# Loading 128 rows in place of 96 for the values of a pair of heads

## The chip, the cores and the metric

The kernel runs on one core of one Trainium2 chip. The metric is the device time of one execution in microseconds (us); a lower time is better. The engines are PE (TensorE, matmuls), PEld (its weight loads), DVE (VectorE), ACT (ScalarE), POOL (GpSimd) and SP (SyncE, which issues all DMA transfers here).

## The reference

Local attention with block summaries, then a feed-forward layer in fp32. Batch 4, 8 heads, 768 tokens, head size 64; 512 model features, 2048 hidden.

```python
k_sum = k.reshape(B, H, nb, block, D).max(axis=3)      # block = 32, nb = 24
v_sum = v.reshape(B, H, nb, block, D).mean(axis=3)
mask_l = np.abs(pos[:, None] - pos[None, :]) < window  # window = 16
scores_s = scale * einsum('bhsd,bhnd->bhsn', q, k_sum) + np.log(block)
a = softmax(concatenate([where(mask_l, scores_l, -1e9), scores_s]))
x = matmul(a, concatenate([v, v_sum]))                 # -> (3072, 512)
h = x @ w_in
g = where(h >= 1, h, where(h <= -1, 0, (h + 1) ** 2 / 4))
out = g @ w_out
```

The weights come as 64-bit floats, 8 MB for each of the two matrices.

## The kernel before

The 3072 tokens are cut into 8 chunks of 384 tokens, c = 0 to 7: two halves for each of the 4 batch entries. Each chunk has 4 pairs of heads, p = 0 to 3. A step is named by a letter and its numbers: v02 is the load of the values of chunk 0, pair 2; F213 is a first-layer product of chunk 2.

For a pair, queries come in blocks of 64, six to a chunk. A block looks at a window of 96 keys (its own 64 and 16 on each side) and at 24 block summaries, 120 in all (KA = 120, KW = 96). The values lie in a tile `v` of 128 partitions by 6 blocks by 128 columns (two heads of 64): partitions 0 to 95 hold the windows and come by a DMA load (load_vals, v, L206 to L208), partitions 96 to 119 hold the 24 means, and partitions 120 to 127 are not read. The means are made on the chip: raw values come by another load (y, L203), DVE sums them (Y, L229), PE turns them (Z, L233), ACT copies them to the first block's columns of partitions 96 to 119 (mean_vals, V, L237), and POOL spreads them over the other five blocks (spread_vals, W, L241). Only then can PE multiply values by weights (values, A, L300). The host lays the windows out in `vwin`, an array of (batch, pair, half, 96, 6, 128) fp32 numbers; a load takes a contiguous piece of 96 rows of 3,072 bytes.

Keys are alike: window keys for chunk 0 are cut on the chip from raw keys (r, L178); for the later chunks they are loaded (k, L184), and POOL writes the summaries beside them (C, L225), so it waits for the load. Scores are S (L253), masks M (L261), exponentials E (L271), reciprocals D (L276), norms N (L281), transposes T (L286), copies of these P (L293), the split of a result into two fp32r parts X and L (L309, L314).

The feed-forward part takes 16 slices of 128 hidden features. Its weights come by 32 loads (w, L105 and L108) of 512 KB; ACT, DVE and POOL convert them to pairs of fp32r numbers (a at L120, b at L125, c at L133 to L141, d at L146 and L148, e at L154). First-layer products are F (L324), the activation G, H, I, J, O (L330 to L349), second-layer products B (L358).

What sets the order: chunk 0, all weight loads and conversions and the scores of chunk 1 are written out by hand as a list of steps (OPENING), which every engine follows. After it, PE's order is given by loops, and the other engines follow a scheduler. `v` tiles have 2 buffers (the loads of pairs 2 and 3 of chunk 0 go to a place in a weight buffer called `first`), so a later load waits until PE has used the values two pairs before. All DMA transfers are issued by SP in one row; the framework gives them eight semaphores in turn (named DMAHW0 to DMAHW7), and each transfer waits for the one eight places before it to land. An instruction that reads or overwrites what a load writes waits for that load's semaphore; regions that don't overlap make no wait.

Of the kernel before, what the change touches and what calls it, by code (L numbers as in the profile page):

```python
# [19 lines left out]
P = 128  # L20
# [4 lines left out]
KW = QB + 2 * WIN  # L25
KA = KW + NSUM
NPAIR = H // 2
T = 384
NHALF = S // T
# [44 lines left out]
def fused_kernel(ctx: ExitStack, tc: tile.TileContext, q2, kT, kwin, vT, vwin, w_in, w_out, mask, ident, out):  # L74
    nc = tc.nc
# [21 lines left out]
    def room(i, what, shape, dtype):  # L97

        return wpool.tile(shape, dtype, tag=f"w{i}", name=f"{what}{i}")
# [58 lines left out]
    q_ts, k_ts, v_ts, s_pss, es, dens, t_pss, pts, vs_pss, o_pss, xs = ({} for _ in range(11))  # L158

    def input_tile(pool, what, shape, c, p):  # L160
        if c == 0 and (what, p) in at_first:
            return at_first[what, p]
        tag, bufs = ("w", W_BUFS) if pool is stage else (what, {"k": K_BUFS, "q": Q_BUFS, "v": 2}[what])
        return pool.tile(shape, F32, tag=tag, name=f"{what}{c}_{p}", bufs=bufs)
# [3 lines left out]
    for i, share in enumerate(FIRST):  # L168
        at, at_room = 0, room(NF - 1 - i, "first", [P, 4 * DM], F32)
# [35 lines left out]

    def load_vals(c, p):  # L206
        v_ts[c, p] = input_tile(load, "v", [P, NB, P], c, p)
        nc.sync.dma_start(out=v_ts[c, p][:KW], in_=vwin[c // NHALF, p, c % NHALF])  # L208

    def window_keys(c, p):  # L210

# [161 lines left out]
    def load_constants():  # L373
# [5 lines left out]

    steps = {  # L380
        "m": load_constants, "r": load_raw_keys, "k": load_keys, "q": load_queries, "y": load_raw_vals, "v": load_vals, "w": fetch,
        "K": window_keys, "R": sum_keys, "C": summary_keys, "S": scores, "M": masks, "E": exps, "D": reciprocals, "N": norms,
        "T": transposes, "P": turned, "Y": sum_vals, "Z": turn_vals, "V": mean_vals, "W": spread_vals, "A": values, "X": high, "L": low,
# [122 lines left out]
```

## Time and profile before

| | |
|---|---|
| median of 3 runs | 663.87 us (662.9 to 664.74) |
| the profiled execution | 663.65 us |
| its span, first to last instruction | 661.8 us |
| busy: PE, ACT, POOL, DVE | 631.8, 370.3, 263.6, 254.9 us |
| granted TensorE clock, mean | 0.992 |
| DMA traffic | 63.55 MB, 96 GB/s over the span |
| loads of values, 288 KB each | 32, two of them to `first` |

The profile shows one execution. Times in it count from its first instruction. A row of a timeline gives start, duration, engine, line, operation, output<-input, count, and in brackets the idle time before it and what ended that wait. A row of the chain gives start, duration and what the time went to. A row of a window gives the window, its length, the busy time of PE, PEld, DVE, ACT and POOL with the count of instructions, the granted clock, the mean busy share of the 16 DMA engines, and GB/s. SPq is SP's own instruction that issues a transfer; the transfer itself lands later.

### The profile page before, as it was taken

The page shows a single profiled execution, that of the slowest core. Times are in us where ns is not written, and L with a number is a line of the kernel's source. Part 1 is how long each engine was busy: PE and PEld are TensorE (multiplying, and loading weights), DVE is VectorE, ACT ScalarE, POOL GpSimd, SP SyncE. Part 2 cuts the span into 40 slices and gives each one's busy share as a digit, 9 for nine tenths or more (in the row PEclk, how much of TensorE's full clock was granted, in tenths as well). Part 3 has the DMA queues.
Part 4 walks back from the last instruction along what each step waited for, and adds up shares of the span by engine and source line. Part 5 has one row for each costly group of instructions (what it writes and reads, how often), then busy time and mean ns, then how long its engine had stood idle before and what let it go on. Part 6 is the DMA issues. An engine that isn't in the chain of part 4 may idle for free.

```text
span 661.8 us, 11703 instructions
## 1 busy us (share of the span) xinstructions
PE 631.8 (95%) x4448; PEld 557.3 (84%) x4448; DVE 254.9 (39%) x494; ACT 370.3 (56%) x948; POOL 263.6 (40%) x300
## 2 busy tenths in 40 slices
PE   3779998899999999999999999999999999999997
PEld 2568787788898888899888888988888998889996
DVE  5879899362123322243222321235222122211111
ACT  3779897454546555464555545565554655544332
POOL 3569888343333332333333233234323323322221
PEclk9979999989999999999999999999999999999999
DMA  9999970370114121062122410254111100000001
GB/s 308 312 307 292 300 225 1 127 209 17 37 53 149 53 53 53 24 216 58 53 53 64 138 29 25 53 169 127 53 53 33 59 19 19 1 37 12 1 1 48
DMA packets 49767, 63.55 MB, mean 96 GB/s; under 512 B 24880, under 2 KB 33328, under 8 KB 49712
## 3 DMA queue, kind: packets, MB, share of 16 engines
q1 hardware_dynamic: 49712, 62.81, 32.0%
q8 instruction: 35, 0.57, 0.4%
q14 instruction: 20, 0.16, 0.1%
HBM read 56.51 MB, written 6.29 MB: 95 GB/s over the span
## 4 chain that ended last, share of the span: by engine, by line
PE 84%; DMA 9%; DVE 4%; ACT 1%; SPq 1%; issue 1%; POOL 0%; DVEq 0%; ACTq 0%
PE h L324 37%; PE acc L358 37%; PE o_ps L300 3%; DMA raw<-in_w_in 3%; PE s_ps L253 3%; PE t_ps L286 3%; DMA first<-in_vwin 2%; DMA q<-in_q 2%; DMA v<-in_vwin 1%; DMA first<-in_kT 1%; DVE w L141 1%; DVE c L133 1%; DVE c L136 1%; SPq L108 0%; DVE t L339 0%
## 5 line engine op out<-in xcount | busy, mean ns | idle before, releaser
L324 PE MATMUL h<-xhi,halves 128*128 128x384 f32 x1024 | 291.2, 343 | 6.6 <-DVE t L339 5.5
L358 PE MATMUL acc<-halves,ghi 128*128 128x512 f32 x768 | 239.8, 394 | 0.0
L349 POOL TENSOR_TENSOR glo<-t,ghi 128x384 fp32r<-128x384 f32 x128 | 129.5, 1013 | 203.2 <-ACT ghi L344 202.4
L324 PEld LDWEIGHTS h<-xhi,halves 128*128 128x128 f32 x1024 | 189.0, 189 | 17.0 <-issue 4.7
L339 DVE SCALAR_TENSOR_TENSOR t<-h,t 128x384 f32<-128x384 f32 x128 | 71.1, 556 | 270.8 <-ACT t L336 263.5
L324 PE MATMUL h<-xlo,halves 128*128 128x384 f32 x512 | 173.2, 338 | 0.0
L358 PEld LDWEIGHTS acc<-halves,ghi 128*128 128x128 f32 x768 | 144.7, 188 | 27.5
L358 PE MATMUL acc<-halves,glo 128*128 128x512 f32 x384 | 153.9, 401 | 0.1
L330 ACT ACTIVATE t<-h,ones_half 128x384 f32<-128x384 f32 x128 | 73.9, 578 | 121.7 <-PE h L324 121.2
L271 ACT ACTIVATE e<-e,den 128x120 f32<-128x120 f32 x192 | 73.4, 384 | 55.6 <-DVE den L266 55.6
L324 PEld LDWEIGHTS h<-xlo,halves 128*128 128x128 f32 x512 | 97.1, 190 | 4.5
L344 ACT CAST ghi<-t 128x384 fp32r<-128x384 f32 x128 | 65.4, 512 | 62.0 <-DVE t L339 61.8
L358 PEld LDWEIGHTS acc<-halves,glo 128*128 128x128 f32 x384 | 72.4, 189 | 12.5 <-issue 0.8
L281 POOL TENSOR_TENSOR e<-e,den 128x360 f32<-128x360 f32 x64 | 49.2, 789 | 56.0 <-ACT t L330 40.1
L336 ACT ACTIVATE t<-t 128x384 f32<-128x384 f32 x128 | 67.2, 526 | 3.6
L154 POOL TENSOR_TENSOR halves<-w,halves 128x1024 fp32r<-128x1024 f32 x16 | 38.5, 2408 | 3.0 <-ACT halves L148 2.1
L225 POOL COPY k<-ks 128x144 f32<-128x144 f32 x30 | 9.1, 305 | 74.5 <-DMA k<-in_kwin 70.6
L241 POOL COPY v<-v 24x640 f32<-24x640 f32 x30 | 21.5, 717 | 43.0 <-issue 33.3
L271 ACT ACTIVATION_READ_ACCUMULATOR e<-e,den 128x1 f32 x192 | 36.1, 188 | 0.0
L314 DVE TENSOR_TENSOR xlo<-o_ps,xhi 128x384 fp32r<-128x384 f32 x32 | 17.7, 554 | 46.4 <-ACT xhi L309 46.4
L300 PEld LDWEIGHTS o_ps<-pt,v 120*64 120x64 f32 x720 | 24.7, 143 | 12.1 <-ACT ghi L344 7.9
L261 DVE SCALAR_TENSOR_TENSOR e<-s_ps,mask_sb 128x360 f32<-128x360 f32 x64 | 30.9, 523 | 7.1 <-PE s_ps L253 6.8
(54 smaller groups left out, 421.2 us busy)
## 6 DMA issues: line engine op xcount, KB each, us to landing
k<-in_kwin SPq DMA_DIRECT2D x28, 360.0 KB, 4.3
v<-in_vwin SPq DMA_DIRECT2D x30, 288.0 KB, 3.1
raw<-in_w_in SPq DMA_DIRECT2D x16, 512.0 KB, 10.2
raw<-in_w_out SPq DMA_DIRECT2D x16, 512.0 KB, 10.1
out<-o SPq DMA_DIRECT2D x24, 256.0 KB, 2.1
q<-in_q SPq DMA_DIRECT2D x56, 96.0 KB, 4.1
kraw<-in_kT SPq DMA_DIRECT2D x13, 384.0 KB, 3.8
vraw<-in_vT SPq DMA_DIRECT2D x13, 384.0 KB, 3.8
```

Source lines behind the costliest of these rows:

```text
L154: nc.gpsimd.tensor_tensor(out=lo, in0=converting[i].bitcast(F32), in1=hi.bitcast(F32), op=ALU.subtract)
L261: nc.vector.scalar_tensor_tensor(out=es[c, p, j], in0=s_pss[c, p][j][:, :NT * KA].rearrange("p (t n) -> p t n", n=KA), scalar=1.0 / math.s ...
L271: nc.scalar.activation(out=e[:, t, :], in_=e[:, t, :], func=AF.Exp, bias=nm[:, t:t + 1], scale=1.0, accum_out=den[:, t:t + 1])
L281: nc.gpsimd.tensor_tensor(out=e, in0=e, in1=den.unsqueeze(2).broadcast_to([P, NT, KA]), op=ALU.mult)
L300: nc.tensor.matmul(o_pss[c, p][j * D:(j + 1) * D, cols], v_ts[c, p][:KA, blk, j * D:(j + 1) * D], pts[c, p, j][:KA, cols], start=True, sto ...
L324: nc.tensor.matmul(hs[c, f][:, :T], weight["win", f][w][:, k * P:(k + 1) * P], x, start=(k == 0 and n == 0), stop=(k == NK - 1 and n == 2))
L330: nc.scalar.activation(out=ts[c, f], in_=hs[c, f][:, :T], func=AF.Relu, bias=ones_half, scale=0.5)
L336: nc.scalar.square(out=ts[c, f], in_=ts[c, f])
L339: nc.vector.scalar_tensor_tensor(out=ts[c, f], in0=hs[c, f][:, :T], scalar=1.0, in1=ts[c, f], op0=ALU.max, op1=ALU.min)
L344: nc.scalar.copy(out=hi, in_=ts[c, f])
L349: nc.gpsimd.tensor_tensor(out=lo, in0=ts[c, f], in1=hi.bitcast(F32), op=ALU.subtract)
L358: nc.tensor.matmul(acc[c][i], a[:, rows], weight["wout", f][w], start=(f == 0 and n == 0), stop=(f == NF - 1 and n == 2))
```

## The change

A load of values now takes 128 rows of the same array in place of 96: the array is read as one list of rows, and the 32 rows behind the wanted 96, the start of the next load's piece, come along. They go to partitions 96 to 127 of the tile. The means then overwrite partitions 96 to 119 as before, and the last 8 partitions are not read. The very last load of the array has no rows behind it and stays at 96.

```diff
     def load_vals(c, p):
         v_ts[c, p] = input_tile(load, "v", [P, NB, P], c, p)
-        nc.sync.dma_start(out=v_ts[c, p][:KW], in_=vwin[c // NHALF, p, c % NHALF])
+        windows = vwin.rearrange("b p h k n d -> (b p h k) n d")
+        at = ((c // NHALF * NPAIR + p) * NHALF + c % NHALF) * KW
+        rows = min(P, windows.shape[0] - at)
+        nc.sync.dma_start(out=v_ts[c, p][:rows], in_=windows[at:at + rows])
```

No instruction changes its place on any engine. Lines behind the change are three further down (L208 becomes L211, L237 becomes L240). What changes in the order are the sizes on SP and some waits. On SP, in the opening, before; the names are output<-input with the size, and in brackets the semaphores that the transfer waits for (v_1 is the load of pair 1, v_0 of pair 0, first_91 of pair 2):

```order
L208 DMA v_1_248<-in_vwin 96x768 [waits DMAHW6_49]
L208 DMA v_0_250<-in_vwin 96x768 [waits DMAHW7_49]
L192 DMA first_87<-in_q 128x768 [waits DMAHW0_49]
L108 DMA raw_253<-in_w_out 128x1024 [waits DMAHW1_49]
L105 DMA raw_253<-in_w_in 128x4x256 [waits DMAHW2_49]
L203 DMA first_89<-in_vT 128x768 [waits DMAHW3_49]
L184 DMA k_0_317<-in_kwin 128x720 [waits DMAHW4_49]
L198 DMA q_0_319<-in_q 64x6x64 [waits DMAHW5_49]
L198 DMA q_0_319<-in_q 64x6x64 [waits DMAHW6_49]
L208 DMA first_91<-in_vwin 96x768 [waits DMAHW7_49]
L108 DMA raw_358<-in_w_out 128x1024 [waits DMAHW0_49]
```

The same place after:

```order
L211 DMA v_1_248<-in_vwin 128x768 [waits DMAHW6_49]
L211 DMA v_0_250<-in_vwin 128x768 [waits DMAHW7_49]
L192 DMA first_87<-in_q 128x768 [waits DMAHW0_49]
L108 DMA raw_253<-in_w_out 128x1024 [waits DMAHW1_49]
L105 DMA raw_253<-in_w_in 128x4x256 [waits DMAHW2_49]
L203 DMA first_89<-in_vT 128x768 [waits DMAHW3_49]
L184 DMA k_0_317<-in_kwin 128x720 [waits DMAHW4_49]
L198 DMA q_0_319<-in_q 64x6x64 [waits DMAHW5_49]
L198 DMA q_0_319<-in_q 64x6x64 [waits DMAHW6_49]
L211 DMA first_91<-in_vwin 128x768 [waits DMAHW7_49]
L108 DMA raw_358<-in_w_out 128x1024 [waits DMAHW0_49]
```

Nothing moved; three loads are larger. The rows also show how a load's landing can be read from SP: the second L198 row waits for the semaphore that v_1 was the last to use, so it is issued when v_1 has landed, the next row when v_0 has landed, and the last row when first_87 has.

On ACT, around the copy of the means of pair 2 of chunk 0 (V02, output first_91), before:

```order
L125 ACTIVATE raw_253<-raw_253 128x1024
L271 ACTIVATE e_3_1_327,den_3_329<-e_3_1_327,den_3_329 128x120 [waits DVE_49,Pool_49]
L271 ACTIVATE e_3_1_327,den_3_329<-e_3_1_327,den_3_329 128x120 x2
L237 ACTIVATE first_91<-vs_ps_2_361 24x128 [waits PE_49]
L293 COPY pt_2_1_393<-t_ps_2_1_369 120x384 [waits PE_49,Activation_49]
L271 ACTIVATE e_3_0_325,den_3_329<-e_3_0_325,den_3_329 128x120 x3
L293 COPY pt_2_0_402<-t_ps_2_0_385 120x384 [waits PE_49,Activation_49]
L125 ACTIVATE raw_358<-raw_358 128x1024 [waits DMAHW1_49,DMAHW0_49]
```

And after:

```order
L125 ACTIVATE raw_253<-raw_253 128x1024
L274 ACTIVATE e_3_1_327,den_3_329<-e_3_1_327,den_3_329 128x120 [waits DVE_49,Pool_49]
L274 ACTIVATE e_3_1_327,den_3_329<-e_3_1_327,den_3_329 128x120 x2
L240 ACTIVATE first_91<-vs_ps_2_361 24x128 [waits DMAHW7_49,PE_49]
L296 COPY pt_2_1_393<-t_ps_2_1_369 120x384 [waits PE_49,Activation_49]
L274 ACTIVATE e_3_0_325,den_3_329<-e_3_0_325,den_3_329 128x120 x3
L296 COPY pt_2_0_402<-t_ps_2_0_385 120x384 [waits PE_49,Activation_49]
L125 ACTIVATE raw_358<-raw_358 128x1024 [waits DMAHW1_49,DMAHW0_49]
```

The copy now also waits for semaphore 7 of the DMA transfers, that of the load of first_91. The copies of means (V) and their spreading on POOL (W) have such a wait in every pair whose load takes 128 rows; the instructions and their order are the same.

## The prediction

> **What bounds the kernel now.** I read the page from the top first: the span, and the forty slices (busy tenths of PE, PE's granted clock, busy tenths of the DMA engines).
>
> ```profile
> span 661.8 us, 11703 instructions
> PE   3779998899999999999999999999999999999997
> PEclk9979999989999999999999999999999999999999
> DMA  9999970370114121062122410254111100000001
> ```
>
> The execution splits in two. For about six slices (16.5 us each) the DMA engines are full and PE is not; after that PE is full and the DMA engines are mostly idle. The windows say it in numbers (PE, PEld, DVE, ACT and POOL busy, then clock, DMA share and GB/s):
>
> ```profile
> 50.00:60.00 10.00, 9.31 (x64) 7.60 (x64) 9.39 (x17) 9.94 (x18) 9.34 (x8) 1.00 1.09 286
> 140.00:580.00 440.00, 440.00 (x3184) 391.60 (x3183) 131.83 (x276) 238.16 (x653) 149.64 (x181) 1.00 0.23 66
> ```
>
> From 140 to 580 us PE is busy 440.00 of 440 us with the DMA engines at 0.23. Nothing that a load costs there can be seen, unless it makes PE wait. The opening is another matter, and the chain that ended last names what paces it:
>
> ```profile
> 4.43 5.68 DMA first<-in_kT
> 10.12 9.79 DMA v<-in_vwin
> 19.92 10.84 DMA first<-in_vwin
> 30.78 10.71 DMA q<-in_q
> ...
> 56.09 10.38 DMA raw<-in_w_in
> ```
>
> Up to 56.09 + 10.38 = 66.47 us the chain is one transfer behind another: each is issued when the one eight places earlier has landed (the waits on eight semaphores in the order rows above), and lands some 10 us later. From there on the chain runs over ACT, DVE and PE. So a load matters to the end if it lies in the queue ahead of the transfer issued at 56.09, and by what it takes of the stream's time there.
>
> **The change part by part.** Every load of values but the very last goes from 96 rows of 3,072 bytes to 128 rows, 98,304 bytes more. No instruction moves on any engine; what is new are the rows and the waits that come of them.
>
> *The stream of the opening.* These rows of SP's timeline give the pace:
>
> ```profile
> 9.46 0.98 SPq L208 DMA_DIRECT2D v<-in_vwin  x2
> 11.11 0.35 SPq L192 DMA_DIRECT2D first<-in_q  x1
> 12.08 0.35 SPq L108 DMA_DIRECT2D raw<-in_w_out  x1
> 13.13 0.38 SPq L105 DMA_DIRECT2D raw<-in_w_in  x1
> 16.08 0.33 SPq L184 DMA_DIRECT2D k<-in_kwin  x1
> 17.63 0.65 SPq L198 DMA_DIRECT2D q<-in_q  x1
> 18.79 0.61 SPq L198 DMA_DIRECT2D q<-in_q  x1
> 19.92 0.88 SPq L208 DMA_DIRECT2D first<-in_vwin  x1
> 20.85 0.91 SPq L108 DMA_DIRECT2D raw<-in_w_out  x1
> 28.41 0.33 SPq L208 DMA_DIRECT2D first<-in_vwin  x1
> 29.76 0.43 SPq L105 DMA_DIRECT2D raw<-in_w_in  x1
> 30.78 1.67 SPq L198 DMA_DIRECT2D q<-in_q  x2
> 36.06 2.62 SPq L208 DMA_DIRECT2D v<-in_vwin  x1
> 46.79 1.06 SPq L208 DMA_DIRECT2D v<-in_vwin  x1
> 57.43 2.05 SPq L208 DMA_DIRECT2D v<-in_vwin  x1
> ```
>
> Six loads of values are issued before 56.09: two from 9.46 (the second at 10.12, by the chain), then 19.92, 28.41, 36.06 and 46.79; the one at 57.43 is behind it. Where SP is blocked, the difference of two issues is the time that one earlier transfer took of the stream. Three loads of 96 rows read this way: 18.79 - 17.63 = 1.16, 19.92 - 18.79 = 1.13 and 30.78 - 29.76 = 1.02 us, mean 1.10. Five loads of 128 rows of the same 3,072 bytes: 11.11 - 10.12 = 0.99, 12.08 - 11.11 = 0.97, 13.13 - 12.08 = 1.05, 17.63 - 16.08 = 1.55 and 20.85 - 19.92 = 0.93, mean 1.10. A third more bytes at the same price: the load of 96 rows does not go at the stream's byte rate. The two ends are these. By bytes, 98,304 at the 286 GB/s of the second window are 0.34 us, times six is 2.1 us more. By the best rows, 0.93 against 1.16, a load gives back 0.23 us, times six 1.4 us less. Two lone transfers, the fastest landings of values and of raw keys, lie between:
>
> ```profile
> DMA to landing us min/median/max: 2.8/3.2/11.5
> DMA to landing us min/median/max: 3.0/3.9/10.9
> ```
>
> That is 0.2 us for the 32 rows, or 1.2 us for six, but there nothing is queued, so it isn't the nearest row; the stream's own pace is. The 1.55 stands behind two weight loads of short pieces, and the other four average 0.985, which is 0.12 less than the 1.10 of a values load, 0.7 us in six. I take the middle between the mean with that row (nothing) and without it (-0.7): -0.35 us at 66.47. The instruction that takes up the chain there is this one on ACT:
>
> ```profile
> 66.55 1.16 ACT L120 ACTIVATE raw<-raw 128x1024 f32<-128x1024 f32 x1 [1.27 <-DMA raw<-in_w_in]
> ```
>
> ACT was idle 1.27 us before it, so all of the 0.35 can be used; beyond 1.27 us ACT's own work would be next.
>
> Here two rules of the Trainium skill speak on opposite sides. SBUF — State Buffer, section Door 1: The DMA port swizzle, has partitions 0 to 63 on eight ports and 64 to 127 on the other eight, eight partitions to a port. By it the busiest ports take eight rows of a 96-row load as of a 128-row one, and the price is nothing; the paces of 1.10 and 1.10 agree. DMA: Bandwidth & Descriptors, section Why a DMA increments its semaphore by 16 and not by 1, says that 96 and 128 partitions both go to 16 engines. By it an engine moves eight rows in place of six, and the price is the byte rate's; that is the first rival, and the paces speak against it.
>
> *The new waits.* The means go to partitions 96 to 119 of the tile, which the load now writes too. So the ACT copy of the means (L237) and POOL's spreading of them (L241) wait for the load. One place is late. The load issued at 19.92 landed at 30.76, and ACT copied its means at 29.21:
>
> ```profile
> 29.21 0.26 ACT L237 ACTIVATE first<-vs_ps 24x128 f32<-24x128 f32 x1
> 31.03 0.46 ACT L293 COPY pt<-t_ps 120x384 f32<-120x384 f32 x1
> 34.08 1.12 ACT L125 ACTIVATE raw<-raw 128x1024 int32<-128x1024 uint32 x1 [2.58 <-DMA raw<-in_w_in]
> 32.10 0.92 PE L300 MATMUL o_ps<-pt,first 120*64 120x64 f32 x24
> 37.02 0.28 PE L233 MATMUL vs_ps<-ident_sb,vs 128*24 128x128 f32 x1 [2.43 <-DVE vs L229]
> 36.01 0.95 DVE L229 TENSOR_REDUCE vs<-first 128x24 f32<-128x768 f32 x1 [1.87 <-DMA first<-in_vT]
> 47.24 0.27 ACT L237 ACTIVATE v<-vs_ps 24x128 f32<-24x128 f32 x1
> ```
>
> ACT now stands for 30.76 - 29.21 = 1.55 us. Behind it are queued two copies of transposes (the second is that of 31.03) and three exponentials, for which DVE's reciprocals, POOL's norms, its spreading and PE's products at 32.10 wait. All of it has cover: ACT then waits 2.58 us for weights, DVE 1.87 us for raw values, PE 2.43 us for DVE. 1.55 is less than each, and each of these waits ends with a transfer that this stall doesn't touch. Priced 0; with the cover gone, 1.55 us. The copy of 47.24 is the next closest: its load was issued at 36.06 and had landed by 46.79, when SP issued the transfer eight places on, so 0.45 us are left there, and a stall only if the stream gets later by more than ACT does. In the steady part the load of one pair's values comes long before: the loads are issued from 9.5 to 548.5 us and the means copied from 19.6 to 584.0, some 35 us between the last of each, where a load lands in about 3.
>
> ```profile
> L208 SPq DMA_DIRECT2D v<-in_vwin x30: 316/333/2619, 9.5 to 548.5; - x30
> L237 ACT ACTIVATE v<-vs_ps x30: 264/265/266, 19.6 to 584.0; 24x128 f32<-24x128 f32 x30
> ```
>
> There the keys' load stands right behind on SP, and POOL's summary of the keys waits for it; it may land 0.2 to 0.34 us later. That price is 0 as long as PE doesn't wait for POOL, and in the window from 140 us it waits for nothing.
>
> *The sum.* The profiled execution took 663.65 us, 661.8 of span and 1.85 around it; 663.65 - 0.35 + 0 + 0 = 663.3. It stood 0.22 us below the median of the three runs, 663.87, so against that median the forecast is 663.5. I give 663.4. About 0.3%, 2.0 us, is what a measurement of this kernel can tell from no change.
>
> **The rivals.** *The rows are paid for at the byte rate.* For it: the DMA share is over 1.0 in the opening and a lone load lands 0.2 us earlier with 96 rows. Against: 1.10 and 1.10. Place: the transfer that lands at 66.47. It gives +2.1 us, 665.6 to 666.0 by the sum and by the median. It becomes slower than the bound once a load costs over 0.33 us of the stream. Chance 0.15, a little under half of it beyond the bound.
>
> *PE's clock is granted otherwise.* Two stretches ran at about half clock, each behind a gap in PE's work (the first behind the 2.43 us above):
>
> ```profile
> 37.60:44.50 6.90, 6.10 (x58) 5.02 (x56) 5.62 (x10) 4.92 (x13) 5.81 (x6) 0.51 1.06 277
> 133.20:136.60 3.40, 3.40 (x12) 3.10 (x11) 3.15 (x5) 2.15 (x8) 2.42 (x3) 0.51 0.90 311
> ```
>
> At 0.51, the 3.40 us of products in the second stretch are some 1.7 us of work, so 1.7 us are lost where PE bounds. The stall moves PE's burst of 32.10 by about 1 us toward the gap that ends at 37.02, and all later work moves by some tenths. If a stretch goes, or the early one costs the chain less, the kernel gains up to 1.7 us, and with the faster stream ends at 661.4 to 661.8: chance 0.13, most of it beyond the bound. If a new stretch comes where PE bounds the kernel, it loses 1.7 us, 665.1: chance 0.09, a third of it beyond the bound with a slower stream on top.
>
> *The full loads gain all that the best rows say.* -1.4 us, cut to 1.27 by ACT: 662.4 to 662.6, within the bound. Chance 0.13. That the change does not do what it says is hardly open: the order rows show 128 rows in all these loads.
>
> **How the numbers follow.** The forecast, within 0.8 us of 663.4, has 0.50; the full gain 0.13; bytes 0.15; the clock 0.13 down and 0.09 up. The range goes from 661.5, the clock's gain, to 665.9, the price by bytes. Faster by over 0.3% (below 661.9): most of the clock's 0.13 and some of the full gain, 0.15. Slower (above 665.9): 0.07 of the bytes, 0.03 of the clock, 0.02 for an uncovered stall, 0.12. The same: 0.73.
>
> **What would show it.** Right: SP's issues from 9 to 57 us about as far apart as now or closer; the chain still transfers up to about 66 us, with ACT's instruction on the weights (L120) at 66.0 to 66.6; a wait of 1 to 2 us of ACT (the copy of means, now three lines lower) for a load of values near 29 us, and an equally shorter wait for weights behind it; PE full from 140 us. Wrong: a values load taking 1.3 us and more of the stream, the chain's first ACT instruction at 68 us, or ACT waiting for values at more than one place, with PE's gaps in the opening longer than before.

## The result, and the profile after

The changed kernel takes 658.38 us (median of 4 runs, 657.72 to 658.90), the kernel before 663.83 beside it (662.90 to 664.74). The ratio is 0.9917, with a 95% interval from 0.9900 to 0.9935: 5.5 us faster, where 0.35 us was forecast, and below the forecast's range, which began at 661.5. The profiled execution agrees: its span is 656.7 us against 661.8, 5.1 us less.

The page of the changed kernel, the rows that answer to those of before (span; busy tenths of PE and of the DMA engines in 40 slices):

```profile
span 656.7 us, 11705 instructions
PE   3789998899999999999999999999999999999997
DMA  9999950542104222261223310163211100010001
```

The DMA engines are full for five slices as before, but in the sixth they are busy five tenths in place of seven. The windows say when the time was gained. First four windows of the kernel before that the prediction didn't show (PE, PEld, DVE, ACT, POOL busy, then clock, DMA share, GB/s):

```profile
10.00:20.00 10.00, 5.75 (x55) 3.81 (x49) 9.29 (x21) 8.11 (x30) 5.23 (x13) 1.00 1.06 336
30.00:40.00 10.00, 6.77 (x91) 5.64 (x90) 7.89 (x16) 7.36 (x25) 4.95 (x7) 0.88 1.08 301
60.00:70.00 10.00, 9.55 (x50) 8.28 (x49) 8.94 (x17) 8.54 (x14) 8.51 (x6) 1.00 1.10 262
80.00:90.00 10.00, 8.51 (x45) 7.30 (x45) 9.79 (x18) 8.46 (x13) 8.94 (x9) 1.00 1.07 364
```

The same windows after, with the one from 50 us and the long one that the prediction gave for before:

```profile
10.00:20.00 10.00, 5.89 (x57) 3.84 (x49) 9.28 (x20) 8.51 (x32) 5.71 (x13) 1.00 1.05 385
30.00:40.00 10.00, 8.43 (x115) 6.58 (x116) 9.06 (x18) 9.44 (x29) 6.83 (x8) 0.92 1.08 334
50.00:60.00 10.00, 9.71 (x68) 8.28 (x67) 9.59 (x18) 9.82 (x21) 9.59 (x8) 1.00 1.08 327
60.00:70.00 10.00, 10.00 (x54) 9.02 (x53) 9.63 (x17) 9.87 (x15) 9.69 (x8) 1.00 1.06 267
140.00:580.00 440.00, 440.00 (x3145) 392.01 (x3144) 128.97 (x273) 237.76 (x652) 149.20 (x180) 1.00 0.23 69
```

At the same DMA share the engines move more: 385 GB/s in place of 336 from 10 us on, 334 in place of 301 from 30, 327 in place of 286 from 50. The bytes that the change adds explain the smaller part of it: two loads between 10 and 20 us bring 0.20 MB more, and 10 us at 49 GB/s more are 0.49 MB. The rest is transfers that come earlier. ACT, which converts the weights, is busy 9.44 and 9.87 us of 10 where it was 7.36 and 8.54. From 140 us on PE is busy 440.00 us of 440 in both kernels: the whole gain is made before.

SP's timeline shows the stream gaining, issue by issue (start, duration, engine, line, operation, output<-input, count):

```profile
16.09 0.33 SPq L184 DMA_DIRECT2D k<-in_kwin  x1
17.10 1.57 SPq L198 DMA_DIRECT2D q<-in_q  x2
19.05 0.33 SPq L211 DMA_DIRECT2D first<-in_vwin  x1
20.02 0.33 SPq L108 DMA_DIRECT2D raw<-in_w_out  x1
...
33.82 2.25 SPq L211 DMA_DIRECT2D v<-in_vwin  x1
...
43.19 1.21 SPq L211 DMA_DIRECT2D v<-in_vwin  x1
...
50.91 1.51 SPq L105 DMA_DIRECT2D raw<-in_w_in  x1
53.83 1.33 SPq L211 DMA_DIRECT2D v<-in_vwin  x1
```

The two first loads of values took 19.05 - 17.10 = 1.95 us of the stream, against 19.92 - 17.63 = 2.29 before, so 0.98 each in place of 1.15. The load of raw values *ahead* of them, 128 rows in both kernels, took 17.10 - 16.09 = 1.01 us against 17.63 - 16.08 = 1.55. And the stream's lead grows over the opening: the loads of values are issued 0.87 us earlier (19.05 against 19.92), then 2.24 (33.82, 36.06), 3.60 (43.19, 46.79) and 3.60 (53.83, 57.43), and the weights that the chain of before ended its transfers with 5.18 us earlier (50.91, 56.09).

What waits for it, ACT, in its timeline (in brackets the idle time before a row, and what ended it):

```profile
29.27 0.26 ACT L240 ACTIVATE first<-vs_ps 24x128 f32<-24x128 f32 x1 [0.75 <-DMA first<-in_vwin]
31.69 1.20 ACT L125 ACTIVATE raw<-raw 128x1024 int32<-128x1024 uint32 x1
61.31 1.13 ACT L120 ACTIVATE raw<-raw 128x1024 f32<-128x1024 f32 x1
```

The row at 61.31 is the instruction that started at 66.55 before, after a wait of 1.27 us (each is the seventh of L120 to start after 30 us, in the same sequence); now it waits for nothing. The chain that ended last says the same as a whole:

```profile
PE 86%; DVE 6%; DMA 3%; issue 2%; ACT 1%; SPq 1%; POOL 1%; DVEq 0%; POOLq 0%; ACTq 0%
```

DMA had 9% of it before, one transfer behind another from 4 to 66 us; now most of those stretches belong to PE, DVE and ACT. Two transfers of weights are still in the chain, later: one from 63.28 to 70.24 us and one from 71.96 to 79.67.

### The profile page after: what moved, and what is told of

It reads as the page before. It is cut to its first block, busy times and chain, and to the rows that moved or that the text cites. A ratio compares the mean times of both kernels' runs of the same rounds, so it can differ in the third digit from the quotient of the medians.

```text
span 656.7 us, 11705 instructions
## 1 busy us (share of the span) xinstructions
PE 629.6 (96%) x4448; PEld 555.6 (85%) x4448; DVE 254.4 (39%) x494; ACT 370.4 (56%) x948; POOL 263.4 (40%) x300
## 4 chain that ended last, share of the span: by engine, by line
PE 86%; DVE 6%; DMA 3%; issue 2%; ACT 1%; SPq 1%; POOL 1%; DVEq 0%; POOLq 0%; ACTq 0%
PE h L327 39%; PE acc L361 37%; PE o_ps L303 3%; PE s_ps L256 3%; PE t_ps L289 3%; DMA raw<-in_w_in 1%; DMA raw<-in_w_out 1%; DVE den L269 1%; DVE e L264 1%; DVE c L133 1%; DVE w L141 1%; DVE c L136 1%; DMA kraw<-in_kT 1%; PE vs_ps L236 1%; SPq L198 0%
```

## The experiments

The theory formed from the two traces: a load of 96 rows delays not only itself but the transfers that are under way beside it, and the opening waits for their sum. Its rivals: the gain comes from something else than the stream (the new waits, PE's clock, later loads), or the stream's gain is in the loads themselves.

A number that the table uses beside the time: the load v20, the first of chunk 2, goes to the tile that held v12, so it waits for PE to have used v12. Its issue on SP marks how far PE has come at about 115 us. In the kernel before it is the first of the two loads of this row:

```profile
115.37 7.16 SPq L208 DMA_DIRECT2D v<-in_vwin  x2
```

v20 is read from one traced execution of each kernel, and the last column gives that execution's own time; the second column is a median. Kernels with the same loads in the opening differ in v20 by 0.32 us (before, and 128 rows behind the opening only) and by 0.45 us (changed, and 128 rows in the opening only), so a smaller difference says nothing. Times beside the kernel before on the same chip:

| kernel | us | before | ratio, 95% interval | v20 issued, us | that execution, us |
|---|---|---|---|---|---|
| before | 663.83 | | | 115.37 | 663.65 |
| changed | 658.38 | 663.83 | 0.9917, 0.9900 to 0.9935 | 110.03 | 658.46 |
| 128 rows in the opening only | 659.04 | 664.38 | 0.9917, 0.9893 to 0.9940 | 109.58 | 658.97 |
| 128 rows behind the opening only | 663.64 | 663.87 | 0.9995, 0.9980 to 1.0010 | 115.69 | 663.45 |
| 128 rows in the first two loads only | 663.76 | 663.87 | 1.0000, 0.9987 to 1.0012 | 114.32 | 662.95 |
| 128 rows in the later five of the opening only | 659.47 | 664.22 | 0.9926, 0.9901 to 0.9950 | 110.65 | 658.92 |
| 112 rows in all | 664.86 | 664.38 | 1.0003, 0.9988 to 1.0018 | 117.44 | 665.19 |
| 120 rows in all | 668.17 | 663.87 | 1.0070, 1.0045 to 1.0096 | 117.70 | 666.04 |
| changed, with full loads of queries | 658.62 | 664.38 | 0.9910, 0.9887 to 0.9934 | 110.38 | 658.84 |
| before, with full loads of queries | 660.10 | 663.87 | 0.9947, 0.9926 to 0.9969 | 112.97 | 662.37 |

**The stream by itself.** A program of loads alone, stage behind stage, eight transfers under way (one execution; the weights blocks are of `w_out`):

```python
stages = [("full", 128, 24, 0), ("rows96", 96, 24, 0), ("rows112", 112, 24, 0), ("rows120", 120, 24, 0),
          ("rows64", 64, 24, 0), ("mix96", 96, 12, 1), ("mix128", 128, 12, 1), ("weights", 0, 0, 24)]
...
nc.sync.dma_start(out=t[:rows], in_=windows[at:at + rows])
```

> This kernel does none of the reference's work: it only issues loads, eight in flight, and a few stores between its eight stages. Stages of 24 loads of the values' rows (3,072 bytes each): 128 rows, 96, 112, 120, 64; then 12 pairs of a 96-row load and a 512 KB weight load, 12 pairs of a 128-row load and a weight load, 24 weight loads. Theory (a load of 96 rows makes DMA engines get in each other's way, on itself and on what is queued beside it): 0.97 to 1.0 us for a load of 128 rows, 1.0 to 1.2 us for one of 96 although it moves a quarter less, 112 rows no better than 128; a pair with 96 rows 2.5 us or more, a pair with 128 rows 2.3 us. Rival (an engine moves its rows one after another, the loads are not the cause): 0.73 us for 96 rows, 0.85 for 112, 0.97 for 128, and the pair with 96 rows 2.0 us, below the pair with 128.

Windows inside its eight stages, in the order of that list (the program uses no engine; the last three columns are clock, DMA share and GB/s):

```profile
5.00:25.00 20.00, 0.00 (x0) 1.00 1.02 391
35.00:55.00 20.00, 0.00 (x0) 1.00 1.03 277
66.00:92.00 26.00, 0.00 (x0) 1.00 1.03 267
104.00:138.00 34.00, 0.00 (x0) 1.00 0.97 229
146.00:168.00 22.00, 0.00 (x0) 1.00 1.03 206
178.00:203.00 25.00, 0.00 (x0) 1.00 1.03 313
214.00:238.00 24.00, 0.00 (x0) 1.00 1.03 400
246.00:273.00 27.00, 0.00 (x0) 1.00 1.03 411
```

Bytes over rate give the pace of one load. 128 rows are 393,216 bytes at 391 GB/s, 1.01 us. 96 rows are 294,912 bytes at 277, 1.06 us: more than the full load takes. 112 rows take 1.29 us, 120 rows 1.61, 64 rows 0.95. A pair of a load of values and a weights block of 524,288 bytes takes 2.62 us with 96 rows (819,200 bytes at 313) and 2.29 with 128 (917,504 at 400). So a full load saves 0.05 us among its like, and 0.33 beside a weights block. Alone, the weights go at 411 GB/s, 1.28 us a block.

Whose time it is can be read from SP, as the prediction read it. In a stage of pairs, a load and a weights block alternate, and each issue waits for the transfer eight places before, one of its own kind, to land. So the step from a load's issue to the next weights issue is what a weights block took, and the step on to the next load is what a load took. With 96 rows, then with 128:

```profile
182.68 0.32 SPq L84 DMA_DIRECT2D mix<-in_vwin  x1
184.28 0.34 SPq L90 DMA_DIRECT2D mix96w<-in_w_out  x1
185.31 0.32 SPq L84 DMA_DIRECT2D mix<-in_vwin  x1
```

```profile
219.04 0.33 SPq L84 DMA_DIRECT2D mix<-in_vwin  x1
220.32 0.33 SPq L90 DMA_DIRECT2D mix128w<-in_w_out  x1
221.29 0.33 SPq L84 DMA_DIRECT2D mix<-in_vwin  x1
```

Beside 96 rows the weights block took 184.28 - 182.68 = 1.60 us and the load 185.31 - 184.28 = 1.03; beside 128 rows 1.28 and 0.97. From the third pair of each stage on, the block takes 1.60 to 1.79 us beside 96 rows against 1.27 to 1.30 beside 128, and the load 0.90 to 1.03 against 0.97 to 1.07. What a 96-row load costs lies in its neighbour's time, and a reading of the load's own landing doesn't see it. That a 96-row load costs by its own bytes, 0.75 of a full one, is refuted. Why such a load holds up its neighbour isn't shown by these runs.

**The opening only, and the rest only.** 128 rows for chunks 0 and 1, then the other half:

```diff
-        rows = min(P, windows.shape[0] - at)
+        rows = P if c < 2 else KW
```

> 128 rows for the loads of chunks 0 and 1 only, 96 for the other 24. Theory: all of the gain is in the opening's queue, so 658.4 us, as the changed kernel. Rival (the steady part gains, by its keys' loads or POOL's waits): 661 us or more.

```diff
-        rows = min(P, windows.shape[0] - at)
+        rows = KW if c < 2 else min(P, windows.shape[0] - at)
```

> 96 rows in the loads of the opening (chunks 0 and 1), 128 in all later ones: the other half of the run in which only the opening's loads had 128 rows. Theory (all of the gain comes in the opening): no change, 663.5 to 664.4 us beside a kernel before of 663.9, with PE busy throughout from 140 us on in both. Rival (later loads, from 105 us on, carry a part): 660 to 663 us.

659.04 and 663.64 us: the gain is the opening's. The loads of the steady part cost or save nothing beyond the interval, from 1.3 us less to 0.7 us more. Chunks 0 and 1 have eight loads; the eighth, v13, is issued at 94.31 us in the kernel before, behind all weights, so the text counts the seven ahead of it.

**112 rows.** The same program as the changed one, with every new wait, 16 rows fewer:

```diff
-        rows = min(P, windows.shape[0] - at)
+        rows = min(112, windows.shape[0] - at)
```

> 112 rows in place of 128 in every load. The load still writes partitions that the means overwrite, so all the new waits stay; each engine moves 7 rows, which again don't fall on it evenly. Theory of the uneven rows: little or no gain is left, 661 to 664 us. Rival (the gain comes from the new waits, which shift ACT and PE and the half-clock stretch): 658.4 us, all of it stays. Rival by rows (the more the better): 660 us.

664.86 us, ratio 1.0003, outside the theory's 661 to 664: no gain is left. The gain doesn't come from the new waits nor from an order of events that they set, since this kernel has them all; and more rows aren't better by themselves. Its v20 is issued 2.1 us later than that of before, and that execution took 1.5 us longer (665.19 against 663.65); the ratio's interval allows 1.2 us. Seven loads at the stream's 1.29 us in place of 1.06 are 1.6 us, but the new waits also weigh more here: up to 60 us ACT waits 3.0 us for loads of values, against 0.8 us in the changed kernel.

**120 rows.** The number of rows that PE reads:

```diff
-        rows = min(P, windows.shape[0] - at)
+        rows = min(KA, windows.shape[0] - at)
```

> All loads of values take 120 rows (24 of the next load's) in place of 128. By the bare stream, where such a load took 1.61 us against 1.07 of 96 rows and 0.98 of 128, the seven loads of the opening take 3.8 us more than those of the kernel before: 666 to 669 us beside a kernel before of 663.9. Rival (the other transfers under way fill the engines that a lagging one leaves idle, so that in the mix only bytes count, or as with 112 rows nothing is seen): 663 to 665 us.

668.17 us (four executions, 666.04 to 669.18), 4.3 us slower than before; the stream's 1.61 us for such a load gave 3.8 (seven loads by 0.55). The size isn't settled: the traced execution is the fastest of the four, 2.4 us slower than that of before, with v20 2.3 us later, and ACT waits 4.8 us for loads of values up to 60 us, so a part may be the new waits'. The direction stands: the kernel is slowed by a load that the bare stream shows slow, and sped up by one that it shows fast.

**The first two loads, and the five others.** The parts of the opening's seven (the second edit also takes in v13, behind the stream):

```diff
-        rows = min(P, windows.shape[0] - at)
+        rows = P if (c, p) in ((0, 0), (0, 1)) else KW
```

> Only the first two loads of values (those that land before 21 us) take 128 rows, the five others of the opening and all later ones 96. Theory (a 96-row load delays itself and the transfers that are under way beside it): the raw values, the two loads and the weights block behind them landed 1.3 us earlier in the changed kernel (24.16 against 25.43 us), and the five other loads keep their price, so about 1 to 1.5 us of the gain: 662.5 to 663.3 us beside a kernel before of 663.9. Rival (the gain needs the later loads, since the conversions catch up with an early lead while VectorE and ScalarE pace them): 663.6 to 664.2 us, no gain. Second rival (the first two set the stream's rhythm, and all else follows): 658 to 660 us.

```diff
-        rows = min(P, windows.shape[0] - at)
+        rows = P if c < 2 and (c, p) not in ((0, 0), (0, 1)) else KW
```

> The other part of the run in which only the first two loads of values had 128 rows: here those two take 96, the five later ones of the opening (landing from 29 us on) 128, and all behind the opening 96. Theory (each 96-row load delays the stream by itself and its neighbours, and the delays add up): all of the gain but the first two's 1.0 to 1.3 us of the stream, so 659.3 to 660.5 us beside a kernel before of 663.9. Rival (the delay comes from a mixture of the two kinds, so that the gain needs all of them, as the first two alone gave nothing that the times show): 662 to 664 us. Second rival (the first two are worth nothing, being made up for later): 658.2 to 659 us.

The five others give 659.47 us, 4.75 less than before, inside what the theory had. The first two give 663.76, no gain within 0.9 us either way: the theory's 1 to 1.5 us didn't come, and the time is the rival's. The trace of the first two shows a lead nevertheless, in the chain and on SP:

```profile
43.32 10.71 DMA raw<-in_w_out
54.05 11.41 DMA raw<-in_w_in
```

```profile
114.32 7.16 SPq L211 DMA_DIRECT2D v<-in_vwin  x2
```

The last transfer of its chain lands at 54.05 + 11.41 = 65.46, 1.01 us before that of the kernel before, and v20 is issued 1.05 us earlier. With the five others:

```profile
110.65 7.14 SPq L211 DMA_DIRECT2D v<-in_vwin  x2
```

4.72 us earlier. 1.05 + 4.72 = 5.77 against 5.34 of the changed kernel (110.03) and 5.79 of the kernel with 128 rows in the opening only: in the opening the parts add up, as closely as v20 can tell. The traced execution with the first two took 662.95 us, 0.7 less than that of before. Whether the rest of the 1.05 us is given back behind 115 us or lies in the spread of the times stays open.

**Full loads of queries.** Queries of the chunks behind the first come in two transfers of 64 rows. One load of 128 rows of 1,536 bytes from a compact array replaces them, first in the changed kernel, then in the kernel before:

```diff
-            for rows in halves_of:
-                nc.sync.dma_start(out=q_t[rows], in_=blocks[rows, :, rows])
+            nc.sync.dma_start(out=q_t, in_=qT[b, p, :, hf * NB:(hf + 1) * NB, :])
```

> The changed kernel, and the queries of chunks 1 to 7 come as one load of 128 rows of 1,536 bytes from an array without the zeros, in place of two loads of 64 rows of six pieces of 256 bytes. Theory: loads of 64 rows are uneven too, and 16 of them are queued in the opening; each pair of them takes about 1.1 us of the stream now and about 0.5 us then, and what stands beside them gets faster: 653 to 656 us. Rival (from 60 us on the conversion of the weights paces the opening, not the queue): 658 us, no change from the changed kernel.

> The kernel before (96 rows), with the queries of the chunks from the second on loaded as one transfer of 128 rows of 1,536 bytes from a compact array, in place of two of 64 rows each. With the changed values this brought nothing. Theory (the opening of the kernel before waits for its stream, and that of the changed kernel no longer does): here it brings something. A pair of half loads takes 1.2 us of the stream (0.82 and 0.43, 0.87 and 0.38), the full load 0.53 with the changed values; three pairs land before 62.5 us, so 2 us and what their neighbours gain: 660.5 to 662.3 us beside a kernel before of 663.9. Rival (the stream of the kernel before wasn't what its end waited for, only its 96-row loads were): 663.4 to 664.4 us.

In the changed kernel this gives 658.62 us, nothing, where the theory had 653 to 656; in the kernel before 660.10, 3.8 us less, a little more than expected (v20 comes 2.4 us earlier in the traced execution, the slowest of six). The stream gets faster in both. The edit changes two things at once, 128 rows in place of twice 64 and pieces of 1,536 bytes in place of 256, so it doesn't tell which of them counts. In the kernel before the opening waits for it: its chain still runs over transfers, the last landing at 50.92 + 12.63 = 63.55 us in place of 66.47.

```profile
38.87 12.04 DMA k<-in_kwin
50.92 12.63 DMA raw<-in_w_in
```

In the changed kernel with full queries the stream runs ahead of what uses it. Windows of that kernel, then SP's waits from 40 to 66 us (line, what it waited for, us in total, times, longest):

```profile
30.00:40.00 10.00, 9.29 (x122) 7.30 (x120) 8.77 (x18) 9.06 (x27) 6.08 (x8) 1.00 1.05 381
40.00:50.00 10.00, 8.49 (x46) 6.94 (x43) 10.00 (x20) 9.00 (x15) 9.70 (x9) 1.00 1.05 381
50.00:60.00 10.00, 9.90 (x69) 8.45 (x69) 9.80 (x19) 9.83 (x21) 9.81 (x8) 1.00 0.90 292
```

```profile
SPq L210 <- PE o_ps L302: 7.7, 1, 7.7
```

The queue goes at 381 GB/s until 50 us, and then SP stands 7.7 us before a load of values, because PE hasn't used the tile that it goes to. DVE is busy 10.00 us of 10 from 40 to 50 us, and PE, DVE, ACT and POOL are each busy 9.80 us or more from 50 to 60. The chain of this kernel holds no transfer between 5 and 90 us, where that of the changed kernel still held the two from 63 to 80, and the time is the same. So 658.4 is about what the opening's own work allows, and a faster stream gains nothing more there.

## Why the prediction was wrong, point by point

**What bounds the kernel** was right: the opening waits for its stream until 66 us, and from 140 us on PE is full. The gain comes in the one and none that shows in the other (659.04 with the opening's loads alone, 663.64 with the others alone).

**The price of a load is the step that failed.** The prediction read what a 96-row load takes of the stream from the distance of two issues, 1.10 us, and compared it with 128-row loads of the same queue, 0.985 without the 1.55 and 1.10 with it; it took the middle, -0.35 us for six loads at the transfer that landed at 66.47. That term measured -5.2: the instruction on ACT that takes it up starts at 61.31 in place of 66.55. A load's own pace was well read: full loads now take 0.98 in place of 1.15, and the bare stream has 1.01 in place of 1.06. What was put at nothing, without a reason, is what such a load costs the transfers around it. The row of 1.55 us was put down to two weight loads behind it, and used as evidence that 128 rows can be dear. It was the neighbour of two 96-row loads: this transfer, 128 rows in every kernel, takes 0.96 to 1.01 us in the four kernels whose first two loads of values have 128 rows, and 1.52 to 1.77 in the four where they have 96. That row was the price, read with the wrong sign. In the bare stream a pair with a weights block costs 0.33 us more with 96 rows, and by the landings it is the block that is late; in the kernel the seven loads cost 5.3 to 5.8 us by v20, 0.5 each for the first two and 0.9 each for the five others. Why it is more in the kernel than in the bare pair isn't settled. That the queries' loads in halves of short pieces hold the stream up as well is shown (3.8 us less without them), and so is that the two gains don't add up (5.5 with one, 3.8 with the other, 5.8 with both).

Two rules of the Trainium skill were weighed at this step. SBUF — State Buffer, section Door 1: The DMA port swizzle, has eight partitions at each port. From it the prediction counted the rows at the busiest port, which gives 64, 96, 112, 120 and 128 rows the same price. The bare stream agrees for 64 and about for 96 (0.95 and 1.06 us beside 1.01) and disagrees for 112 and 120 (1.29 and 1.61); the measurement decides. By DMA: Bandwidth & Descriptors, section Why a DMA increments its semaphore by 16 and not by 1, 96 and 128 partitions both go to 16 engines; the price by bytes that was derived from it is refuted by the same rows.

The views of before had a hint. At a DMA share of 1.06 to 1.10 the windows went from 262 to 364 GB/s: the busy share says that engines have transfers under way, not that these go at full pace. The window of 262 has a load of values (57.43) and behind it half loads of queries among its weights; in the one of 364 weights land behind each other.

**The bound at 1.27 us** failed with it. "Beyond 1.27 us ACT's own work would be next" holds only if ACT's earlier work doesn't move. It moved, since ACT waited earlier too, for the same stream and for PE. Its waits of before from 30 to 67 us, line by line:

```profile
ACT raw L125 <- DMA raw<-in_w_in: 2.6, 1, 2.6
ACT t L330 <- PE h L324: 2.0, 1, 2.0
ACT raw L120 <- DMA raw<-in_w_in: 1.3, 1, 1.3
ACT xhi L309 <- PE o_ps L300: 0.5, 1, 0.5
```

And after:

```profile
ACT t L333 <- PE h L327: 0.5, 1, 0.5
ACT raw L125 <- DMA raw<-in_w_in: 0.4, 1, 0.4
```

6.4 us of waiting became 0.9, and the instruction at 66.55 comes 5.24 us earlier, at 61.31. Of the 6.4 us, 3.9 were waits for weights and 2.5 for PE, which shrank with them. The room was up to 6.4 us and not the last wait's 1.27.

**The new wait** was right in its place and in being covered: ACT's copy of the means waits 0.75 us for its load near 29 us (1.55 was worked out and 1 to 2 named as a sign; the load itself lands earlier now), and the conversion of weights behind it starts at 31.69, 2.39 us before its old time. No other instruction on ACT waits for a load of values.

**The steady part** costs nothing that shows, as forecast: 663.64 us with the later loads alone.

**The rivals.** By bytes (665.6 to 666.0): refuted by the result, and by 96 and 128 rows in the bare stream. (The 286 GB/s of its price is that of the first window that the prediction shows, not the second.) PE's clock: there are still two stretches at about half clock, one longer than before:

```profile
21.40:31.60 10.20, 7.79 (x77) 6.38 (x81) 8.33 (x19) 7.96 (x25) 6.57 (x7) 0.50 1.07 344
127.20:130.60 3.40, 3.40 (x12) 3.40 (x11) 3.37 (x6) 1.97 (x9) 1.76 (x2) 0.50 0.94 291
```

The second is as long as it was, and the first went from 6.9 to 10.2 us in a place where PE has time to spare (7.79 us busy of 10.20), so the gain doesn't come from there. The times say so too: the fastest execution of the kernel before on record took 661.89 us, the slowest of the changed kernel 658.90, both at a mean granted clock of 0.996. The full gain (-1.4, cut to 1.27) had the right sign, and the size that the failed step gave it.

## What to carry to other kernels

In a queue with several transfers under way, price a transfer by what the whole stretch takes with it and without it, neighbours counted, and not by the distance to its own landing; a neighbour that takes 1.55 us where its like take 1.0 is a sign. Compare GB/s of windows at the same busy share: this queue went at 262 to 336 GB/s in places where weights alone go at 411. A load of 128 rows with the rest thrown away can be cheaper than one of 96, 112 or 120, and once the stream is ahead of the engines, a further gain there is worth nothing.

## What the runs showed of the hardware that was not expected

- Pace of a load of rows of 3,072 bytes, eight under way, in one execution of the bare stream: 0.95 us for 64 rows, 1.06 for 96, 1.29 for 112, 1.61 for 120, 1.01 for 128. The time doesn't rise with the bytes; 128 rows go faster than 96, 112 or 120.
- A weights block of 512 KB takes 1.28 us alone and beside loads of 128 rows; beside loads of 96 rows it takes 1.60 to 1.79, while the load itself (0.90 to 1.03) takes about what one of 128 rows does (0.97 to 1.07).
- The DMA share stood at 1.03 in the stage of 64-row loads, which moved 206 GB/s, and in that of weights, which moved 411: it can't tell one from the other.
